# A transformer block on one core: QKV products in the score banks, paired rests, a third w1 buffer and first loads from two queues

## The chip, the cores and the metric

The kernel runs on one core of one Trainium2 chip. The metric is the device time of one execution in microseconds. Engines are called PE or TensorE (matmuls), DVE or VectorE, ACT or ScalarE, POOL or GpSimd, and SP or SyncE, which issues the transfers (DMAs).

## The reference

One block on x of shape (1, 2048, 576) in bfloat16: an attention part with 32 heads of 18 columns and a compressive memory, then a feed-forward part of 4608 columns, both on a layer norm and both added to their input.

```python
x = A_x
h = x + attention(layernorm(x), wq, wk, wv, wo, beta)
h2 = h + (gelu(layernorm(h) @ w1 + b1) @ w2 + b2)

# attention: 4 segments of 512 tokens, one after the other, per head
p = softmax(q k^T * scale + causal mask)            # inside the segment
a_dot = p @ v
a_mem = (phi(q) @ M) / (phi(q) @ z + 1e-6)          # phi(t) = t + 1 if t > 0 else exp(t)
o = sigmoid(beta) * a_mem + (1 - sigmoid(beta)) * a_dot
M += phi(k)^T @ v;  z += sum(phi(k))                # for the segments to come
return o @ wo
```

## The kernel before

The 2048 tokens are cut into 16 tiles of 128, and these into eight chunks of two tiles (`NCH`, `c`; a tile is `t = 2 * c + tl`). Two chunks are one segment. The work stands in streams, written as Python generators:

- `stream_P(tl)`: loads x, layer norm, transpose to `xT`, products with `wqkv` (576 rows, 1728 columns, resident), copies out of PSUM to `qk_pad` and `v_aug`, transposes to `QT` and `KT`. From chunk 1 on the 1728 columns are cut into four of 432 (`CH`). Each product sums over 576 rows in five matmuls, four of 128 rows (`mm5`, line 612) and a rest of 65 rows (64 and a row of zeros, line 613).
- `stream_M`: phi(k) with v into the memory (line 799).
- `stream_A`: 80 visits. A visit computes 16 score matmuls of 32 rows, four at a time in the array (line 841), into the four banks of `st4`; one exp over all 2048 columns on ScalarE (line 847); a causal mask; then attention with v into the bank `ox` (line 873, four column tiles). The memory's part is line 910.
- `stream_B(tl)`: transposes the attention's output, product with `wo_t`, adds x, layer norm, transposes to `xn2T` (four buffers of one chunk), and writes h plus b2 to DRAM.
- `stream_F1`: for each chunk nine groups of 512 columns of w1. The rest of 64 rows goes first, as tails in two row halves (line 1185), then four 128-row matmuls each (line 1198). Line 1208 on VectorE or line 1206 on ScalarE adds b1, line 1220 is GELU on ScalarE. Chunk 0's first five groups go by half chunks (lines 1158 and 1160; `xz` holds rows padded with zeros).
- `stream_F2`: 36 matmuls of 288 columns for each half tile (line 1254), then the sum with h (line 1258) and the store.

PSUM has eight banks: four for the scores (`st4`), `ox`, and three small ones (`bank_slots`) that all other products share. When the scores are done, all eight are for F1 and F2.

The weights w1 don't stay on chip. Each group (512 KB and two rests of 32 KB) is loaded anew for each chunk, into two buffers, `w1_bufs`, in turn. For chunk 0 three more lie in the second `hT` buffer, and late in the kernel three lie in `wqkv`.

```python
w1_at = {n: ("w1m", n % 5) if n < NG and n % 5 > 1 else ("w1", n % 5 if n < NG else (n - NG) % 2) for n in range(W1Q)}
```

What runs when is not left to a scheduler at run time. Each operation is recorded with `op(engine, duration, issue, reads, writes)`; `either` names two engines that could do it. The list `ORDER` (written out, from a search by a planner with costs and due times that stands in the same file) gives the order in which all operations are issued, and with a minus sign the second engine of an `either`. `PLACE` gives the small bank of each use. Each engine runs its own queue in this order and waits where data are not there, so nothing overtakes a waiting instruction on its engine. All transfers are issued by SyncE in this kernel, the first loads too (lines 531 to 535: x, then wk, beta, wq, wv).

At the start, before the first product, TensorE runs small matmuls on zeros (line 1326). The transposes of the first tiles are line 657, the product that spreads the gate beta over the partitions is line 550, and the copy of `xT` out of PSUM is line 692.

## Time and profile before

| what | value |
| --- | --- |
| time before, median of 3 runs | 460.34 us (458.75 to 461.04) |
| the profiled execution: its time, its span | 458.34 us, 456.6 us |
| TensorE busy | 448.5 us, 98% of the span |
| ScalarE, VectorE, GpSimd busy | 69%, 63%, 32% |
| mean DMA rate | 183 GB/s |
| granted TensorE clock | 1.00 |

The span runs from the first to the last instruction of one execution; all rows of the profile are from that execution. In a timeline's row the first number is the start in us, the second the length, then engine, line, operation and tiles, with a count of merged instructions; in brackets stands the idle time before it and what ended it. In a row of a group the numbers behind the bar are the busy time, the mean length of one in ns, and the idle time before.

### The profile page before, as it was taken

Reading aid. Unit: us, or ns where it says so; the run is one execution under the profiler, and the core shown is the slowest. Engines: PE = TensorE matmul, PEld = TensorE weight load, DVE = VectorE, ACT = ScalarE, POOL = GpSimd, SP = SyncE. Lnnn points to the kernel's source line nnn. Section 1 sums busy time; section 2 is a strip of 40 time slices with the busy share of each in tenths; the row PEclk is TensorE's granted clock in tenths of the full one; section 3 lists DMA queues with packets and bytes.
Section 4 is the critical chain, followed back from the end, with each engine's and each line's share of the span. In section 5 each row is a group of like instructions: output and inputs, shape, how many; then the busy total and the mean of one; then the engine's idle time right before and its main releaser. Section 6 shows DMA issues by size and latency. Waiting matters only on the chain.

```text
span 456.6 us, 14417 instructions
## 1 busy us (share of the span) xinstructions
PE 448.5 (98%) x6074; PEld 333.2 (73%) x6074; DVE 286.9 (63%) x761; ACT 315.3 (69%) x316; POOL 147.4 (32%) x202
## 2 busy tenths in 40 slices
PE   7999999999999999999999999999999999999997
PEld 5776776666777777776567777667788888888874
DVE  6998888887786767876765686678672532211101
ACT  5999889976887965797786876978932354366230
POOL 4776423564373033436512333233210020000000
PEclk9999999999999999999999999999999999999999
DMA  7989998969798987787796679987778767575001
GB/s 227 329 252 264 193 184 201 182 176 178 166 251 156 232 202 178 195 177 135 204 176 165 180 194 165 201 201 156 192 193 213 196 194 191 161 208 157 27 14 39
DMA packets 137491, 83.39 MB, mean 183 GB/s; under 512 B 72786, under 2 KB 135634, under 8 KB 137426
## 3 DMA queue, kind: packets, MB, share of 16 engines
q1 hardware_dynamic: 137426, 82.47, 76.5%
q8 instruction: 47, 0.77, 0.7%
q14 instruction: 18, 0.15, 0.1%
HBM read 59.43 MB, written 6.49 MB: 144 GB/s over the span
## 4 chain that ended last, share of the span: by engine, by line
PE 89%; DMA 5%; SPq 3%; ACT 1%; DVE 1%; issue 1%; ACTq 0%
PE bank L1254 21%; PE bank L1198 17%; PE bank L612 13%; PE late L1254 6%; PE late L1198 6%; PE st L841 5%; PE ox L873 4%; PE bank L613 3%; PE bank L1185 3%; PE bank L1158 2%; PE ox L1254 1%; PE ox L1198 1%; SPq L367 1%; DMA hT<-in_B_w_dram 1%; DMA w1g<-in_B_w_dram 1%; DMA beta_row<-in_A_beta_dram 1%
## 5 line engine op out<-in xcount | busy, mean ns | idle before, releaser
L847 ACT ACTIVATE pt<-st 128x2048 bf16<-128x2048 f32 x80 | 150.1, 1877 | 41.9 <-PE st L841 21.2
L1254 PEld LDWEIGHTS <-hT 128*128 128x128 bf16 x1152 | 109.4, 98 | 29.6 <-issue 0.8
L1254 PE MATMUL bank<-w_sb,hT 128*128 128x288 bf16 x864 | 126.3, 286 | 0.0
L1198 PE MATMUL bank<-xn2T,w1g 128*128 128x256 bf16 x656 | 85.3, 273 | 0.0
L852 POOL TENSOR_SCALAR_AFFINE_SELECT pt<-pt 128x512 bf16<-128x512 bf16 x81 | 52.4, 658 | 95.2 <-ACT pt L847 88.8
L1198 PEld LDWEIGHTS <-w1g 128*128 128x128 bf16 x768 | 71.4, 98 | 16.2 <-issue 6.1
L1208 DVE TENSOR_TENSOR hT<-bank,b1T 128x512 bf16<-128x512 f32 x70 | 47.3, 685 | 41.5 <-PE bank L1198 41.1
L1220 ACT ACTIVATE hT<-hT 128x1536 bf16<-128x1536 bf16 (+3 forms) x24 | 65.7, 2768 | 0.2
L612 PE MATMUL bank<-wqkv,xT 128*128 128x432 bf16 (+1 forms) x268 | 57.1, 336 | 0.9 <-DMA xT<-xn 0.8
L612 PEld LDWEIGHTS <-xT 128*128 128x128 bf16 x400 | 36.9, 97 | 19.8 <-DMA xT<-xn 0.9
L1206 ACT ACTIVATE hT<-late,b1T 128x256 bf16<-128x256 f32 x32 | 13.3, 477 | 38.7 <-PE late L1198 22.3
L1258 DVE TENSOR_TENSOR ot<-bank,hc 128x288 bf16<-128x288 f32 x24 | 11.0, 456 | 43.0 <-PE bank L1254 38.0
L1206 ACT ACTIVATE hT<-bank,b1T 128x256 bf16<-128x256 f32 x56 | 23.5, 473 | 20.1 <-PE bank L1198 20.1
L1254 PE MATMUL late<-w_sb,hT 128*128 128x288 bf16 (+1 forms) x216 | 33.9, 296 | 0.0
L841 PE MATMUL st<-QT,KT 32*128 32x128 bf16 x1280 | 32.4, 217 | 0.5 <-issue 0.5
L841 PEld LDWEIGHTS <-KT 32*128 32x128 bf16 x1280 | 18.7, 92 | 15.2 <-issue 11.9
L1198 PEld LDWEIGHTS <-wqkv 128*128 128x128 bf16 x272 | 26.0, 98 | 4.6 <-issue 0.8
L854 DVE TENSOR_TENSOR pt<-pt,causal 128x512 bf16<-128x512 bf16 x47 | 22.4, 479 | 8.3 <-ACT pt L847 8.1
L646 POOL TENSOR_TENSOR rstd_b<-rstd_b,mhalf 128x1 f32<-128x1 f32 x16 | 9.3, 582 | 56.2 <-DVE rstd_b L636 53.8
L873 PE MATMUL ox<-pt,v_aug 128*32 128x128 bf16 x1184 | 26.3, 221 | 0.0
L873 PEld LDWEIGHTS <-v_aug 128*32 128x32 bf16 x1184 | 17.2, 96 | 10.6 <-issue 8.2
L613 PE MATMUL bank<-wqkv,xT 65*128 65x432 bf16 (+1 forms) x67 | 22.6, 338 | 0.0
(156 smaller groups left out, 642.0 us busy)
## 6 DMA issues: line engine op xcount, KB each, us to landing
w1g<-in_B_w_dram SPq DMA_DIRECT2D x50, 512.0 KB, 4.1
wqkv<-in_B_w_dram SPq DMA_DIRECT2D x17, 512.0 KB, 3.9
w_sb<-in_B_w_dram SPq DMA_DIRECT2D x6, 864.0 KB, 7.7
hd<-h_t SPq DMA_DIRECT2D x14, 288.0 KB, 4.2
hc<-hd SPq DMA_DIRECT2D x28, 144.0 KB, 2.9
w1g<-in_B_w_dram SPq DMA_DIRECT2D x100, 32.0 KB, 3.2
x_b<-in_A_x_dram SPq DMA_DIRECT2D x18, 144.0 KB, 3.0
hT<-in_B_w_dram SPq DMA_DIRECT2D x5, 512.0 KB, 6.0
```

Of the source, the lines that this page charges most:

```text
L612: nc.tensor.matmul(out=out_ap, lhsT=lhsT_of(slice(0, P), k), rhs=rhs_of(slice(0, P), k), start=(k == 0), stop=False)
L613: nc.tensor.matmul(out=out_ap, lhsT=lhsT_of(slice(0, KTAIL), 4), rhs=rhs_of(slice(0, KTAIL), 4), start=False, stop=True)
L841: nc.tensor.matmul(out=st4[:, i, n * P:(n + 1) * P], lhsT=KTs[(c - c % 2 + kt // 2) % 3][rows, g, (kt % 2) * P:(kt % 2 + 1) * P], rhs=QTs[ ...
L847: op("ACT", 1.88, lambda: nc.scalar.activation(out=pt[:], in_=st4[:], func=ACT.Exp, scale=scale), sk, [("pt", slot, n) for n in range(4)], ...
L852: either(("POOL", 0.64, lambda part=part: nc.gpsimd.affine_select(out=part, in_=part, pattern=[[0, 4], [1, P]], compare_op=ALU.is_ge, fill ...
L854: ("DVE", 0.42, lambda part=part: nc.vector.tensor_tensor(out=part, in0=part, in1=causal[:].unsqueeze(1).to_broadcast([P, 4, P]), op=ALU.m ...
L873: nc.tensor.matmul(out=ox[32 * i:32 * i + 32, g % 4 * P:(g % 4 + 1) * P], lhsT=v_flat[(2 * s0 + kt) % 6][:, h * E:h * E + 32], rhs=pts[slo ...
L1198: nc.tensor.matmul(out=bank(b)[:, a * Q:(a + 1) * Q], lhsT=w1_main(wt)[:, k, (2 * (h % 2) + a) * P:(2 * (h % 2) + a + 1) * P], rhs=xn2T[c ...
L1206: nc.scalar.activation(out=hT[:, f + a, :], in_=bank(b)[:, a * Q:(a + 1) * Q], func=ACT.Identity, bias=b1T[:, f + a:f + a + 1])
L1208: either(("DVE", 0.69, lambda hT=hT, f=f, b=b: nc.vector.tensor_tensor(out=hT[:, f:f + 2, :], in0=bank(b)[:].rearrange("p (a w) -> p a w", ...
L1220: op("ACT", (f1 - f0) * Q * 0.00083 + 0.18, lambda hT=hT, f0=f0, f1=f1: nc.scalar.activation(out=hT[:, f0:f1, :], in_=hT[:, f0:f1, :], fun ...
L1254: nc.tensor.matmul(out=acc, lhsT=hT[:, q, tl * P:(tl + 1) * P], rhs=w2_sb[:, q, hs], start=(q == 0), stop=(q == NF - 1))
```

## The change

1. From chunk 3 on (`PAIRED`), the QKV product of a tile takes the four score banks instead of four uses of small banks. The rests come first: four matmuls of 64 rows, on the lower and the upper partitions in turn, so that two use different halves of the array. For this, two DMAs copy 64 rows of `wqkv` to the upper partitions for two of the four cuts, and the layer norm writes the last 64 columns twice. `BEFORE` names the visit ahead of which each tile's product stands.
2. A third buffer for w1 (`w1_bufs`). To make room, `xn2T` goes from four buffers to three, and `beta_row`, `ones`, `b1_rows` and `xz` lie in `t1` and `t2`, which are used later.
3. The first loads may be issued by SyncE or ScalarE (`dma_two`); wq, wk and wv come in halves of 288 columns.
4. A new `ORDER` and `PLACE`. In it ScalarE issues five loads: the first x, the last rows of wq, beta, one half of wq and one of wk.

When the scores are done, the score banks and `ox` now join the small banks at places that `PLACE` gives.

The diff, without `ORDER`, `PLACE` and renamed keys:

```diff
+    def dma_two(kb, issue, rd=(), wr=(), slack=0.0):
+        o = either(("SP", 0.5, lambda: issue(nc.sync)), ("ACT", 0.55, lambda: issue(nc.scalar)), rd, wr, slack)
...
-    w1_bufs = [sbuf(f"w1g{j}", [W1]) for j in range(2)]
+    w1_bufs = [sbuf(f"w1g{j}", [W1]) for j in range(3)]
-    xn2T = [sbuf(f"xn2T{j}", [KT, Q]) for j in range(4)]
+    NX = 3
+    xn2T = [sbuf(f"xn2T{j}", [KT, Q]) for j in range(NX)]
+    early = t1[:].rearrange("p h e -> p (h e)").bitcast(BF16)
+    ones, beta_row, b1_rows = early[:, 0:P], early[:, P:P + H], early[:, 2 * P:3 * P]
+    xz = t2[:].rearrange("p h e -> p (h e)").bitcast(BF16)[:, 0:2 * Q].rearrange("p (h q) -> p h q", h=2)
...
-        weights(wqkv, slice(j * D, (j + 1) * D), W, f"wqkv{j}")
+        for h in range(2):
+            to = slice(j * D + h * HALF, j * D + (h + 1) * HALF)
+            dma_two(290, lambda e, to=to, h=h, W=W: e.dma_start(
+                out=wqkv[:, 0:4, to], in_=W[0:512, h * HALF:(h + 1) * HALF].rearrange("(k p) n -> p k n", p=P)), (), [f"wqkv{j}{h}"])
...
+    PAIRED = 3
+    BEFORE = {6: 22, 7: 23, 8: 27, 9: 38, 10: 45, 11: 47, 12: 52, 13: 55, 14: 62, 15: 64}
...
+            if (c, tl) == (PAIRED, 0):
+                yield need(lambda: (PAIRED - 1, 0) in half_V and (PAIRED - 1, 1) in half_V, idle=False)
+                for lo, hi in ((CH, 2 * CH), (3 * CH, 4 * CH)):
+                    dma(55, lambda lo=lo, hi=hi: nc.sync.dma_start(out=wqkv[64:P, 4, lo:hi], in_=wqkv[0:64, 4, lo:hi]),
+                        [f"wqkv{j}t" for j in range(3)], ["wqkv_pad"])
...
+            paired = c >= PAIRED
+            if paired:
+                yield need(lambda: visited[0] >= BEFORE[t] and all(u in projected for u in BEFORE if u < t), st_slots, [kx] + every, mode=64)
+                st = st_slots.take()
+                def rests(xTt=xTt, cuts=cuts):
+                    for i, (lo, hi) in enumerate(cuts):
+                        rows = slice(64 * (i % 2), 64 * (i % 2) + 64)
+                        nc.tensor.matmul(out=st4[:, i, 0:hi - lo], lhsT=xTt[rows, 4, :], rhs=wqkv[rows, 4, lo:hi], start=True, stop=False,
+                                         skip_group_check=True)
+                op("PE", 2 * mm(CH), rests, [kx] + every, [st], n=8, mode=64)
...
+                    for k in range(4):
+                        nc.tensor.matmul(out=area()[:, 0:hi - lo], lhsT=xTt[:, k, :], rhs=wqkv[:, k, lo:hi], start=False, stop=(k == 3),
+                                         skip_group_check=True)
...
-    w1_at = {n: ("w1m", n % 5) if n < NG and n % 5 > 1 else ("w1", n % 5 if n < NG else (n - NG) % 2) for n in range(W1Q)}
+    w1_at = {n: ("w1m", n % 6) if n < NG and n % 6 > 2 else ("w1", n % 6 if n < NG else n % 3) for n in range(W1Q)}
```

More of the change, by code (lines that the diff above doesn't have):

```diff
@@ L517, in swap @@
         for i in range(4):
-            banks["st", i] = pool.tile([P, 512], F32, name=f"late{i}")
+            banks["bank", 3 + i] = pool.tile([P, 512], F32, name=f"late{i}")
+        banks["bank", 7] = ox
     bank_slots.free.append("ox")
@@ L834, in scores @@
         own = 2 * (c % 2) + qt
-        sk = [("st", i) for i in range(4)]
+        st = st_slots.take()
+        sk = [st]
         def go():
@@ L1002, in stream_A @@
                             done_A.add(c)
-        bank_slots.free.append("ox")
-        st = [("st", i) for i in range(4)]
-        op("POOL", 0.0, swap, (), st, slack=-1000, port=False)
-        bank_slots.free += st
+        more = [("bank", 3 + i) for i in range(5)]
+        used = [("pt", slot, n) for slot in range(2) for n in range(4)] + [("v", t, j) for t in (2, 3) for j in range(2)]
+        op("POOL", 0.0, dynamic_swap, used, ["ox"] + more, slack=-1000, port=False)
+        bank_slots.free += more
         late.append(True)
```

125 lines of the change are left out of this document (74 added, 51 removed), and 230 rows, old and new, of the table ORDER.

## The prediction

> **What bounds the kernel now.** I read the page's engine table and chain first, then busy time by stretches, then TensorE's timeline around the places that the change touches, then single groups of instructions.
>
> ```profile
> span 456.6 us, 14417 instructions
> PE 448.5 (98%) x6074; PEld 333.2 (73%) x6074; DVE 286.9 (63%) x761; ACT 315.3 (69%) x316; POOL 147.4 (32%) x202
> PE 89%; DMA 5%; SPq 3%; ACT 1%; DVE 1%; issue 1%; ACTq 0%
> ...
> core 0: us, PE busy (x) PEld busy (x) DVE busy (x) ACT busy (x) POOL busy (x), PEclk, DMA share, GB/s
> 0.00:20.00 20.00, 17.68 (x186) 13.12 (x187) 15.45 (x52) 14.46 (x26) 11.52 (x24) 1.00 0.89 271
> ...
> 200.00:240.00 40.00, 38.36 (x619) 26.09 (x617) 27.70 (x76) 33.20 (x33) 17.28 (x22) 1.00 0.83 179
> 240.00:280.00 40.00, 40.00 (x547) 30.08 (x545) 27.55 (x70) 30.14 (x26) 13.21 (x20) 1.00 0.67 174
> ```
>
> TensorE is busy 448.5 of 456.6 us, carries 89% of the chain, and has stretches with no gap at all (240 to 280). No other engine passes 69%. So the time is TensorE's own work plus the few places where it waits. An edit is worth what it takes from one of these two; a faster copy or transfer elsewhere is worth nothing by itself. Busy time hides what a matmul really occupies, because matmuls overlap; I take the distance from one start to the next:
>
> ```profile
> 117.23 0.40 PE L841 MATMUL st<-QT,KT 32*128 32x128 bf16 x16
> 117.56 0.41 PE L873 MATMUL ox<-pt,v_aug 128*32 128x128 bf16 x16
> 117.91 0.39 PE L1185 MATMUL bank<-xn2T,w1g 64*128 64x256 bf16 x4
> 118.23 1.92 PE L1198 MATMUL bank<-xn2T,w1g 128*128 128x256 bf16 x16
> 119.99 0.89 PE L612 MATMUL bank<-wqkv,xT 128*128 128x432 bf16 x4
> 120.72 0.35 PE L613 MATMUL bank<-wqkv,xT 65*128 65x432 bf16 x1
> 120.90 0.89 PE L612 MATMUL bank<-wqkv,xT 128*128 128x432 bf16 x4
> 121.63 0.35 PE L613 MATMUL bank<-wqkv,xT 65*128 65x432 bf16 x1
> 121.91 0.63 PE L873 MATMUL ox<-pt,v_aug 128*32 128x128 bf16 x32
> ```
>
> A full 432-column matmul occupies 0.73/4 = 0.18 us (119.99 to 120.72), and the rest of the contraction, with 65 rows, just as much: 0.18 us (120.72 to 120.90). A 256-column one takes 1.76/16 = 0.11 us (118.23 to 119.99). The four tails of 64 rows, in two row halves, take 0.32 us (117.91 to 118.23): two times 0.11 and 0.10 over, so the halves do run together and the change of tile shape costs 0.10. The other way it costs the same: 121.63 + 0.18 = 121.81, and the next shape starts at 121.91.
>
> **Rests as row pairs.** Of 16 token tiles, the ten of chunks 3 to 7 change. Each had four rests of 0.18 us; now two pairs: 10 x 2 x 0.18 = 3.6 us less. But the pairs stand in a shape of their own. In the order of instructions of the two built programs I count 278 changes of shape before and 296 after, everything counted: 18 more, at 0.10 to 0.12 us each (the upper end from the 16 scores, 0.33 us, of which four times half of 0.11 are streaming) 1.8 to 2.2, taken 2.0. Net 1.6 us less. All of this is on the path, since TensorE has no idle time to hide it in.
> The Trainium skill, "TensorEngine Tiling (Array Packing)", section "Tiling Modes", says that changing the tiling mode drains TensorE; this speaks against pairs in small groups, and the trace agrees, with 0.10 us. Its page "TensorE: Matmul & The Clock Gate", section "Single matmul latency", puts a drain at about 175 ns; an estimate from that page would charge 18 x 0.175 = 3.2 us and leave 0.4 us of the gain. The measured row decides.
>
> **Products in the score banks.** Each paired tile takes all four score banks: 2 x 0.18 + 4 x 0.73 = 3.3 us of products, then five copies out. Until the last copy no scores may be issued, and TensorE takes its queue in order.
>
> ```profile
> L847 ACT ACTIVATE pt<-st 128x2048 bf16<-128x2048 f32 x80 | 150.1, 1877 | 41.9 <-PE st L841 21.2 <-PE ox L873 13.1 <-issue 1.8
> L1220 ACT ACTIVATE hT<-hT 128x4608 bf16<-128x4608 bf16 x10 | 40.1, 4039 | 0.1
> L711 DVE CAST qk_pad<-bank 128x432 bf16<-128x432 f32 x16 | 9.7, 604 | 4.4 <-PE bank L613 4.2
> L710 ACT CAST v_aug<-bank 128x432 bf16<-128x432 f32 x7 | 3.7, 525 | 0.5 <-PE bank L613 0.5
> L1208 DVE TENSOR_TENSOR hT<-bank,b1T 128x512 bf16<-128x512 f32 x70 | 47.3, 685 | 41.5 <-PE bank L1198 41.1 <-ACT pt L847 0.2
> ```
>
> The products finish 0.73 us apart and a copy takes 0.52 (ScalarE) or 0.60 (VectorE), so after the last product one copy, about 0.7 us with its hand-over, is left when its engine is free. In the new order the shortest work between the last product and the next scores is 1.7 us (tile 7: eight matmuls of F2, four tails, 16 of attention; tile 12 much the same), elsewhere 2.1 to 6. I cost it at nothing; the cover is that work, 1.0 us more than needed. If it is gone (a 4.04 us GELU or one 0.69 us eviction ahead of the copy), each tile loses up to 4.04 + 0.52 - 1.7 = 2.9 us: a rival below. On the gain side three small banks, freed of 40 projections, wait less; TensorE's waits on banks are too small now to price, so that stays at nothing.
>
> **Third buffer.** TensorE's waits on transfers after the start are these:
>
> ```profile
> 76.62 0.39 PE L1185 MATMUL bank<-xn2T,hT 64*128 64x256 bf16 x4
> 77.42 1.92 PE L1198 MATMUL bank<-xn2T,hT 128*128 128x256 bf16 x16 [0.40 <-DMA hT<-in_B_w_dram]
> ...
> 148.19 0.66 PE L612 MATMUL bank<-wo_t,xT 128*128 128x288 bf16 x4 [0.30 <-DMA xT<-o_nat]
> ...
> 216.09 0.90 PE L612 MATMUL bank<-wqkv,xT 128*128 128x432 bf16 x4 [0.77 <-DMA xT<-xn]
> ...
> 239.43 0.39 PE L1185 MATMUL bank<-xn2T,w1g 64*128 64x256 bf16 x4 [0.88 <-DMA w1g<-in_B_w_dram]
> ...
> w1g<-in_B_w_dram SPq DMA_DIRECT2D x50, 512.0 KB, 4.1
> ```
>
> The first and last are w1: 0.40 + 0.88 = 1.3 us. With two buffers a load starts when the group two back is done; with three it has a whole group more, against 4.1 us to landing. I take both as gone. Bounds: 0 (the load is late because SyncE issues it late, behind others in its queue, which no buffer cures) to 2.4 us (the two xT waits, 1.07, go too). What is late next is an xT transpose on the same queue. The price of the buffer, one xn2T fewer, is nothing: by the new order the chunk whose buffer is reused has ended its F1 at least 60 us of TensorE work earlier. The same for xz, ones, beta and b1 rows that now lie in t1 and t2: the last read of xz stands 12 us of TensorE work ahead of chunk 2's first memory product, whose result overwrites it. A second small VectorE operation for each of ten layer norms is off the path (63% busy).
> Two added copies on chip put the weights of every second rest on the upper partitions. The second is the 67th transfer of SyncE's new queue; in the old one, issues 67 to 71 run as follows:
>
> ```profile
> 68.51 0.59 SPq L1105 DMA_DIRECT2D hT<-in_B_w_dram  x1
> ...
> 71.72 0.43 SPq L1105 DMA_DIRECT2D hT<-in_B_w_dram  x1
> ...
> 71.72 5.66 DMA hT<-in_B_w_dram
> ```
>
> The first rests come about 75 us in, by the new order's TensorE work ahead of them and the 8 us that the old trace had lost by then. Issued at 68.5 to 71.7, the copy lands with the last row's 5.66 us at 77.4 at the latest: a single wait of 0 to 2.4 us, and I take 0.4, since it is a tenth of that row's 512 KB.
>
> **First loads from two queues.**
>
> ```profile
> 0.79 1.28 ACT L593 ACT_TABLE_LOAD   x1 [0.79 <-PEq L1370]
> 0.80 0.87 SPq L531 DMA_DIRECT2D x_p<-in_A_x_dram  x2
> 1.71 0.43 SPq L534 DMA_DIRECT2D wqkv<-in_A_wk_dram  x1
> 3.09 0.82 DVE L622 BATCH_NORM_STATS2 stats_p<-x_p 128x6 f32<-128x288 bf16 x2 [0.38 <-DMA x_p<-in_A_x_dram]
> 5.53 0.69 ACT L692 COPY xT<-ox 128x640 bf16<-128x640 bf16 x1 [1.01 <-PE ox L657]
> 7.00 0.17 PE L550 MATMUL bank<-beta_row,ones 1*128 1x32 bf16 x1 [0.21 <-DMA beta_row<-in_A_beta_dram]
> 7.50 0.65 PE L612 MATMUL bank<-wqkv,xT 128*128 128x288 bf16 x4
> 10.22 0.36 PEld L612 LDWEIGHTS <-xT 128*128 128x128 bf16 x4 [0.41 <-DMA wqkv<-in_A_wq_dram]
> ```
>
> xT is ready at 6.2 us (5.53 + 0.69), but the first product starts at 7.50: the gate's small product waits ahead of it for beta, whose load stands behind 576 KB of wk. In the new order beta is ScalarE's third issue, and wq comes in halves on both queues. New limit: ScalarE issues five loads (0.43 each, like SyncE's), the fifth once the first x has landed (3.1), to 3.5; then the 1.28 table load, a 0.3 copy, and xT at 5.5 to 6.2 as before. The transposes may be some 0.4 later, as two x loads now share the engines from the start. First product at about 6.7: 0.8 us less. Bounds: a loss of 0.5, if wq's first half lands late, to a gain of 1.3.
> The Trainium skill, "DMA: Bandwidth & Descriptors", section "Issuing engines are not separate DMA queues", says that issuing from several engines saves issue time only. The first 20 us here are busy by 0.89 on the transfer engines at 271 GB/s, which leaves little beyond issue and order; by that rule alone the head would give nothing.
>
> **The sum.** 456.6 - 3.6 + 2.0 - 1.3 + 0.4 - 0.8 = 453.3 us of span. The profiled execution took 458.34 us, 1.74 more than its span, so 455.0; it ran 2.0 under the median of 460.34, so on the median's scale **457.0 us**, 0.7% less. About 0.5%, 2.3 us, is what can be told from no change: 458.0 and 462.6 are the bounds.
>
> **Rivals.** *Gains eaten by the feeds.* The w1 waits turn into others of the same size on SyncE's one queue, and the head stays bound by bytes: 456.6 - 1.6 + 0.4 = 455.4, on the median's scale 459.1, no change. For it: SyncE's queue is in order, and the head's transfers are at 0.89. Against it: the 1.3 us at the head were order (beta), not bytes. 0.20.
> *Late copies hold the score banks: slower.* Place: the scores after each of the ten projections. It decides from 0.6 us a tile on: the forecast is 3.3 under before, 2.3 over is slower, 5.6/10. With 0.9 lost a tile, 453.3 + 9 = 462.3, on the median's scale 466.0. For it: one late copy stops all of TensorE, and the new ScalarE order puts GELUs of 4 us ahead of copies of several tiles. Against it: most tiles have 2 to 6 us of cover, and now TensorE waits little for 80 exps of 1.88 us in the same banks. 0.15.
> *The pairs don't overlap*, both halves reading one at a time: 3.6 back, 460.2, no change. The tails' 0.32 us speaks against it. 0.02.
>
> **How the numbers follow.** Forecast 0.63, of which 0.58 lies under 458.0 and the rest just above, where the head's loss or the full wait for the copy would put it; the first rival, 1.1 above the bound, adds 0.04 to faster. Faster 0.62, same 0.23, slower 0.15. Downward the head can give 0.5 more, the waits 1.1, the shapes 0.2 and the copy 0.4, 2.2 in all, and the lowest of the runs shown (458.75) lies 1.6 under the median: 457.0 - 3.8 = 453.2. Upward I reach past the first rival to the second with 0.5 lost a tile: 457.0 + 5 = 462.0. Range 453.2 to 462.0.
>
> **What would show it.** Right: rests in groups of four with 0.36 us and a change of about 0.10 on each side; 80 scores that start without idle time behind the projections; no TensorE wait on w1 over 0.3 us; the first product before 7 us. Wrong: TensorE idle ahead of scores, put down to a copy from the score banks; idle time of over 1.5 us in any stretch that is full now; a first product after 7.5.

## The result, and the profile after: slower by 0.9%

| | before | after |
| --- | --- | --- |
| median of 13 runs each, same chip | 459.94 us (458.47 to 463.53) | 464.69 us (462.21 to 466.5) |
| ratio after to before, 95% interval | | 1.0092 (1.0065 to 1.0119) |
| span of the profiled execution | 456.6 us | 463.4 us |
| idle gaps of TensorE over 0.02 us, with 1.9 to 2.0 at the start, summed from the trace | 5.4 us | 11.3 us |

457.0 was forecast, with a range of 453.2 to 462.0: the time lies above the range, on the other side of no change. Ratios and their intervals are of the fast runs alone: of the twelve runs each of item 13, its sibling and item 15 below, three, one and two lie over 1.5% above the fastest and are left out there, but not of the medians. In the page of the changed kernel (engines' busy time, then the shares of the chain that ended last) TensorE is as busy as before, in a span 6.8 us longer (4.75 us by the medians: the execution profiled before ran 1.6 us under its median, the one after 0.4 over), and the chain runs through ScalarE and VectorE for 3% each instead of 1%:

```profile
span 463.4 us, 14374 instructions
PE 448.6 (97%) x6067; PEld 331.1 (71%) x6067; DVE 287.8 (62%) x772; ACT 313.8 (68%) x305; POOL 154.3 (33%) x209
PE 85%; DMA 6%; ACT 3%; DVE 3%; SPq 2%; issue 1%; POOL 0%; ACTq 0%; DVEq 0%
```

What TensorE waited for in the changed kernel (sum in us, times, longest):

```profile
PE bank L1245 <- DMA w1g<-in_B_w_dram: 2.1, 2, 1.1
PE bank L1386 <- DVE pq L581: 1.9, 1, 1.9
PE st L895 <- ACT qk_pad L731: 1.6, 2, 1.0
PE bank L1258 <- DMA w1g<-in_B_w_dram: 1.2, 1, 1.2
PE st L895 <- ACT v_aug L731: 1.2, 2, 1.0
PE st L743 <- ACT pt L901: 0.9, 1, 0.9
PE st L743 <- DMA wqkv<-wqkv: 0.7, 1, 0.7
```

L895 is the scores, L743 the paired rests, L1245 and L1258 the first layer's tails and main matmuls, L731 the copies out of the score banks; L1386 is the wait at the very start, 2.0 before. So 2.8 us are scores that stand behind copies, 3.3 us are waits for first-layer weights (1.3 before), 0.7 is the on-chip copy of `wqkv`, and 0.9 is tile 9's rests, which need the score banks that an exponential is still reading.

One more cost stands in no wait of TensorE. The last sum of the feed-forward part, before and after:

```profile
453.93 0.31 DVE L1258 TENSOR_TENSOR ot<-ox,h_t 128x144 bf16<-128x144 f32 x1 [0.49 <-PE ox L1254]
```

```profile
460.03 0.61 DVE L1318 TENSOR_TENSOR ot<-late,h_t 128x432 bf16<-128x432 f32 x1 [1.79 <-PE late L1314]
```

The new order ends with the wider of two pieces, 432 columns and not 144. From the start of this sum to the end of the span it is 3.4 us, before 2.7. These 0.7 us are in the profile of every version with the new order (3.3 to 3.4 us).

The copies, at tile 12, first on TensorE:

```profile
222.19 0.54 PE L743 MATMUL st<-wqkv,xT 64*128 64x432 bf16 x4
222.66 3.09 PE L763 MATMUL st<-wqkv,xT 128*128 128x432 bf16 x16
225.59 0.44 PE L852 MATMUL bank<-v_aug,phik_pad 128*128 128x76 bf16 x8
...
226.71 0.63 PE L928 MATMUL ox<-pt,v_aug 128*32 128x128 bf16 x32
228.36 0.40 PE L895 MATMUL st<-QT,KT 32*128 32x128 bf16 x16 [1.02 <-ACT qk_pad L731]
```

The four rests take 0.47 us with their change of shape (222.19 to 222.66), as forecast. The products end at 225.6. The copies of ScalarE and of VectorE in the same stretch:

```profile
225.79 0.52 ACT L731 CAST qk_pad<-st 128x432 bf16<-128x432 f32 x1 [3.15 <-PE st L763]
226.98 0.28 ACT L731 CAST v_aug<-st 128x144 bf16<-128x144 f32 x1 [0.68 <-DVE v_aug L732]
227.79 0.52 ACT L731 CAST qk_pad<-st 128x432 bf16<-128x432 f32 x1 [0.52 <-DVE qk_pad L732]
```

```profile
226.34 0.61 DVE L732 CAST v_aug<-st 128x432 bf16<-128x432 f32 x1 [2.07 <-ACT qk_pad L731]
227.30 0.46 DVE L732 CAST qk_pad<-st 128x288 bf16<-128x288 f32 x1 [0.35 <-ACT v_aug L731]
```

Two things are to be seen. The first copy starts 0.2 us after the last product, although the first product was done 2.2 us earlier. And each copy begins 0.03 us after the other engine's copy has ended, and names it as its releaser: five copies on two engines run as one chain of 2.5 us. In the ten tiles the copies end 2.4 to 4.1 us after the last product; the scores stand idle at four of them (0.97 us at tile 7, 0.21 at 8, 1.02 at 12, 0.62 at 13).

The first products:

```profile
5.40 0.71 PE L670 MATMUL ox<-ident,xn 128*128 128x128 bf16 x5 [0.52 <-DVE xn L641]
...
7.01 1.16 PE L625 MATMUL bank<-wqkv,xT 128*128 128x288 bf16 x4
...
8.74 1.16 PE L625 MATMUL bank<-wqkv,xT 128*128 128x288 bf16 x4
...
9.94 0.72 PE L625 MATMUL ox<-wqkv,xT 128*128 128x288 bf16 x4
```

The first starts at 7.01, 0.49 sooner than before. But four matmuls take 1.16 us where they took 0.65, half the rate, so the third product starts at 9.94, against 8.73 before.

### The profile page after: what moved, and what is told of

Read it like the earlier page. It is cut to its first block, busy times and chain, and to the rows that moved or that the text cites. A ratio compares the mean times of both kernels' runs of the same rounds, so it can differ in the third digit from the quotient of the medians.

```text
span 463.4 us, 14374 instructions
## 1 busy us (share of the span) xinstructions
PE 448.6 (97%) x6067; PEld 331.1 (71%) x6067; DVE 287.8 (62%) x772; ACT 313.8 (68%) x305; POOL 154.3 (33%) x209
## 4 chain that ended last, share of the span: by engine, by line
PE 85%; DMA 6%; ACT 3%; DVE 3%; SPq 2%; issue 1%; POOL 0%; ACTq 0%; DVEq 0%
PE bank L1314 20%; PE bank L1258 16%; PE bank L625 6%; PE late L1258 6%; PE st L895 5%; PE st L763 5%; PE ox L1314 5%; PE ox L928 4%; PE late L1314 4%; PE bank L1245 3%; DMA w1g<-in_B_w_dram 2%; PE bank L1217 2%; DMA o_col<-oT 2%; ACT pt L901 2%; PE bank L626 2%; DMA wqkv<-wqkv 1%
## 5 line engine op out<-in xcount | busy, mean ns | idle before, releaser
L1314 PE MATMUL bank<-w_sb,hT 128*128 128x288 bf16 x792 | 115.7, 286 | 0.5 <-DVE hT L1268 0.5
L1258 PE MATMUL bank<-xn2T,w1g 128*128 128x256 bf16 x680 | 88.2, 273 | 1.2 <-DMA w1g<-in_B_w_dram 1.2
L1258 PEld LDWEIGHTS <-w1g 128*128 128x128 bf16 x816 | 75.8, 98 | 17.7 <-issue 4.8
L907 POOL TENSOR_SCALAR_AFFINE_SELECT pt<-pt 128x512 bf16<-128x512 bf16 x75 | 48.7, 663 | 74.9 <-ACT pt L901 72.3
L1266 ACT ACTIVATE hT<-bank,b1T 128x256 bf16<-128x256 f32 x48 | 20.2, 475 | 24.7 <-PE bank L1258 24.6
L895 PE MATMUL st<-QT,KT 32*128 32x128 bf16 x1280 | 32.2, 216 | 3.0 <-ACT qk_pad L731 1.6
L763 PE MATMUL st<-wqkv,xT 128*128 128x432 bf16 x160 | 32.5, 346 | 0.0
L895 PEld LDWEIGHTS <-KT 32*128 32x128 bf16 x1280 | 19.2, 92 | 16.8 <-issue 13.3
L625 PEld LDWEIGHTS <-xT 128*128 128x128 bf16 x240 | 22.9, 99 | 8.6 <-ACT xT L713 0.2
L1268 DVE TENSOR_TENSOR hT<-late,b1T 128x512 bf16<-128x512 f32 x16 | 10.9, 686 | 28.7 <-PE late L1258 28.7
L1314 PE MATMUL ox<-w_sb,hT 128*128 128x288 bf16 x180 | 27.9, 286 | 0.0
L1314 PE MATMUL late<-w_sb,hT 128*128 128x288 bf16 (+2 forms) x180 | 27.1, 286 | 0.0
L1258 PEld LDWEIGHTS <-wqkv 128*128 128x128 bf16 x240 | 23.0, 98 | 4.1 <-issue 0.6
L1115 POOL TENSOR_TENSOR h_t<-h_t,b_bc 128x576 f32<-128x576 f32 x16 | 20.6, 1290 | 12.3 <-DVE r L989 8.9
```

The source lines that it names most:

```text
L625: nc.tensor.matmul(out=out_ap, lhsT=lhsT_of(slice(0, P), k), rhs=rhs_of(slice(0, P), k), start=(k == 0), stop=False)
L763: nc.tensor.matmul(out=area()[:, 0:hi - lo], lhsT=xTt[:, k, :], rhs=wqkv[:, k, lo:hi], start=False, stop=(k == 3), skip_group_check=True)
L895: nc.tensor.matmul(out=st4[:, i, n * P:(n + 1) * P], lhsT=KTs[(c - c % 2 + kt // 2) % 3][rows, g, (kt % 2) * P:(kt % 2 + 1) * P], rhs=QTs[ ...
L907: either(("POOL", 0.64, lambda part=part: nc.gpsimd.affine_select(out=part, in_=part, pattern=[[0, 4], [1, P]], compare_op=ALU.is_ge, fill ...
L1258: nc.tensor.matmul(out=bank(b)[:, a * Q:(a + 1) * Q], lhsT=w1_main(wt)[:, k, (2 * (h % 2) + a) * P:(2 * (h % 2) + a + 1) * P], rhs=xn2T[c ...
L1266: nc.scalar.activation(out=hT[:, f + a, :], in_=bank(b)[:, a * Q:(a + 1) * Q], func=ACT.Identity, bias=b1T[:, f + a:f + a + 1])
```

## The experiments

Ratios are to the kernel before, run on the same chip beside each, with 95% intervals; a point is 0.01 of the ratio, 4.6 us. Two kernels' ratios differ reliably only by 0.4 points or so. Line numbers in edited kernels are 16 or 17 higher, since the list `ORDER` takes more lines. The letters of theories are explained in each expectation; from item 9 on E stands for the one queue that weights and transposes share.

**1 and 2. Five copies from one tile or from four.** A small kernel: 24 rounds of four products and of the changed kernel's copies, alternating engines. They differ in this:

```diff
-    one = ps.tile([P, 4, 512], F32, name="one")
-    area = lambda i: one[:, i, 0:432]
+    tiles = [ps.tile([P, 512], F32, name=f"t{i}") for i in range(4)]
+    area = lambda i: tiles[i][:, 0:432]
```

> A small kernel of its own: 24 rounds of four products of 4x432 columns into four banks that are declared as one tile, and the same five copies as the changed kernel's, handed in turn to ScalarE and VectorE. It leaves out everything else of the computation. Theory 'in series' (two reads of one declared tile wait for each other although they are in different banks): a VectorE copy begins only after the ScalarE copy before it has ended, by 0.03 us as in the changed kernel's trace, so a round's five copies take the sum of their times, 0.52 + 0.61 + 0.28 + 0.46 + 0.52 = 2.4 us. Rival 'side by side' (the waits in the changed kernel come from what else the two engines do): the copies of ScalarE and VectorE overlap and a round's copies are over in 1.2 to 1.4 us.

> The same small kernel, with the four banks declared as four tiles of one bank each; nothing else differs. Theory 'in series': now the copies of the two engines overlap, a round's five copies are over in 1.2 to 1.4 us after its last product, and the first of them begin while products still run. Rival 'side by side': no difference between this kernel and the one with one tile.

With one tile, ScalarE, VectorE and TensorE:

```profile
49.49 0.52 ACT L46 CAST qk<-one 128x432 bf16<-128x432 f32 x1 [4.91 <-PE one L43]
50.69 0.40 ACT L48 CAST qk<-one 128x288 bf16<-128x288 f32 x1 [0.68 <-DVE va L47]
51.76 0.28 ACT L50 CAST va<-one 128x144 bf16<-128x144 f32 x1 [0.68 <-DVE qk L49]
```

```profile
50.04 0.61 DVE L47 CAST va<-one 128x432 bf16<-128x432 f32 x1 [5.77 <-ACT qk L46]
51.12 0.61 DVE L49 CAST qk<-one 128x432 bf16<-128x432 f32 x1 [0.47 <-ACT qk L48]
```

```profile
44.63 4.76 PE L43 MATMUL one<-w,xa 128*128 128x432 bf16 x16 [2.70 <-ACT va L50]
52.09 4.54 PE L43 MATMUL one<-w,xa 128*128 128x432 bf16 x16 [2.70 <-ACT va L50]
59.33 3.08 PE L43 MATMUL one<-w,xa 128*128 128x432 bf16 x16 [2.69 <-ACT va L50]
```

With four tiles, ScalarE, then VectorE:

```profile
43.67 0.40 ACT L48 CAST qk<-t 128x288 bf16<-128x288 f32 x1 [1.58 <-PE t L43]
43.97 0.29 ACT L50 CAST va<-t 128x144 bf16<-128x144 f32 x1
45.13 0.52 ACT L46 CAST qk<-t 128x432 bf16<-128x432 f32 x1 [0.88 <-PE t L43]
```

```profile
44.35 0.61 DVE L47 CAST va<-t 128x432 bf16<-128x432 f32 x1 [2.44 <-PE t L43]
44.87 0.60 DVE L49 CAST qk<-t 128x432 bf16<-128x432 f32 x1
```

"In series" holds. From one tile, five copies take 2.55 us end to end (49.49 to 52.04), and TensorE stands idle for 2.70 us in each round. From four tiles the two engines overlap, each copy waits only for its product, some run while TensorE's products do (41.96 to 45.04), and its idle time is 0.48 us a round. The rounds differ by more than that, 7.46, 7.24 and 5.77 us in turn against 3.56, since two of three rounds of the first kernel also run in part at half rate (4.76 and 4.54 us of products, against 3.08). The TensorE rows show why the copies cannot come earlier either: the next round's first product, into a bank that was the first to be read out, waits 2.70 us for the last copy of another bank. Here what is declared as one tile is one resource. I didn't declare the score banks as four tiles in the changed kernel itself: that its copies are a chain for this reason is read from the same hand-overs of 0.03 us. The Trainium skill, "PSUM — Partial Sum Buffer", section "PSUM bank collisions raise a hardware error", asks for a guard by bank and quadrant only; with four tiles the waits agree with that, with one tile they go further.

**3. One copy instead of five** (the rest of q, k and v from chunk 3 on is not brought out).

```diff
+                skip = c >= PAIRED and ch > 0
-                either(("ACT", ..., lambda: nc.scalar.copy(out=dst, in_=src())),
+                either(("ACT", ..., lambda: None if skip else nc.scalar.copy(out=dst, in_=src())),
```

> The changed kernel with four of the five copies out of the score banks left out in each of its ten paired tiles (only the first 432 columns are copied; the rest of q, k and v from chunk 3 on is not brought out). Theory A (the scores wait for the five copies, 2.82 us of idle TensorE before four tiles' scores, each gap costing some 0.25 us more than the record shows): those four gaps go, and the span falls by 2.8 to 4 us, to 459.4 to 460.6. Rival B (the late first-layer weights set the time, and the score gaps only take up slack that would show elsewhere): the gaps go but the next wait for weights grows by as much, and the span stays above 462.4.

Span 459.5, median 461.22, ratio 1.0038 (1.0012 to 1.0064): 0.54 points less, 2.5 us. The four score gaps are gone. Not all of the span's 3.9 us is theirs: the third product started at 8.70 here (1.2), and one wait for weights grew from 0.99 to 1.92, after which the clock stood at 0.50 from 140.4 to 143.8. So theory A holds, with some of it given back to the weights. The edit also takes 40 copies of 0.3 to 0.6 us off ScalarE and VectorE, so the 2.5 us need not all be the scores'; item 5 keeps the copies.

**4. TensorE busy until the first transposes.**

```diff
         for o in arranged():
-            o.issue()
+            for again in range(5 if o.made == 89 else 1):
+                o.issue()
```

> The changed kernel with one of its warm-up matmuls issued five times instead of once, so that TensorE is busy from 4.5 to 5.4 us where it now stands idle between its 13th warm-up and the first transposes (4.68 to 5.40). Theory C (the idle stretch is why the first products run at 240 ns a matmul until 9.9 us, where the kernel before has 120 ns from 5.9 us on): the 120 ns spacing begins by about 6 us, the first product takes 0.6 instead of 1.2 us, the third product starts at 8.3 to 8.6 instead of 9.94, and the span falls by 1.3 to 1.6 us. Rival D (the slow spacing comes from the weights still landing, or from loads issued by ScalarE): the spacing stays 240 ns until 9.9 us and the span does not move.

```profile
5.53 0.48 PE L686 MATMUL ox<-ident,xn 128*128 128x128 bf16 x5
...
6.80 0.66 PE L641 MATMUL bank<-wqkv,xT 128*128 128x288 bf16 x4
...
7.70 0.65 PE L641 MATMUL bank<-wqkv,xT 128*128 128x288 bf16 x4
...
8.45 0.66 PE L641 MATMUL ox<-wqkv,xT 128*128 128x288 bf16 x4
```

In this execution the full rate is there from the transposes on, as theory C has it. Its size was wrong: ratio 1.0085 (1.0060 to 1.0110), median 462.84, only 0.07 points. The profiles of the other runs tell why. With the idle stretch the third product starts at 9.94, 8.70, 8.94, 8.41, 8.42, 8.42 and 8.48 (the changed kernel and the runs of items 3, 5, 6, 8, 9 and 14), mean 8.76; with it filled, at 8.41 to 8.97, mean 8.62 in eight runs; and in the kernel before at 8.73, and at 8.41 in item 10. The profiled execution of the changed kernel was the worst draw. Nor is the idle stretch shown to be the cause: of the seven executions with it four run the first product at the full rate (0.66 us, items 6, 8, 9 and 14), and of the eight without it one doesn't (0.81 us, item 15). The Trainium skill, "TensorE: Matmul & The Clock Gate", section "What's actually happening", says that the rate doubles after a busy window of about 3.4 us that runs freely, so that the onset varies by some 0.5 us. The trace agrees that it varies, but by more: here the full rate comes between 6.75 (or sooner) and 10 us.

**5. Copies on one engine, with cover.**

```diff
-  ORDER: copies of tiles 7, 8, 12, 13 in turn on ScalarE and VectorE;  774 (scores) ... 728 ... 731;  1699 (scores), 1315
+  ORDER: all of them on ScalarE;                                       728, 731, 774;               1315, 1699
```

> The changed kernel with the copies of tiles 7, 8, 12 and 13 all handed to ScalarE and three pieces of feed-forward work put ahead of the scores that stood idle (two of 0.43 us at tile 7, one of 0.47 us at tile 12); all of the computation stays. Theory A (the scores wait for copies that end 2.4 us and more after the last product): a chain on one engine goes every 0.41 us instead of 0.55 to 0.64, so the copies end 0.4 us sooner, and with the cover the idle time before these scores falls from 2.82 to about 1 us; the span falls by 1.5 to 2.2 us from 463.4. Rival B (that idle time is slack against the weights): it falls as much, but the span by under 0.5 us.

Ratio 1.0064 (1.0039 to 1.0088), median 462.70, span 459.9. No score gap is left. 0.28 points, 1.3 us, lie just under A's 1.5 to 2.2 and within what two ratios can differ by chance; 1.0 of the span's 3.5 us is the start (third product at 8.94). The waits for weights stayed (1.21, 1.61, 0.70).

**6 and 7. Five transfers earlier, alone and with 4 and 5.**

```diff
-  ORDER: 500 ... 520 ... 598 ... 519 ... 597 (on-chip copy) ... 531;      967 ... 968;    983 ... 981 ... 982
+  ORDER: 500, 597 ... 520, 519 ... 598, 531;                              967, 968;       983, 982 ... 981
```

> The changed kernel with five transfers put earlier in SyncE's queue: the second on-chip copy of the projection weights right behind the first's neighbours (60.9 instead of 72.9 us), two main loads of first-layer weights at 65 and 67 instead of 70.4 and 73.5, a tail load at 124.9 instead of 138.2, and one at 137 instead of 147.5, each behind the last reader of what it overwrites. Theory B (these loads were given late places in the queue, long after their buffer was free): the idle times of TensorE for weights at 74.94, 142.18 and 153.00 (3.29 us) and for the on-chip copy at 77.99 (0.66) go, and the span falls by 3 to 4 us. Rival E (the transfers are slow because the DMA engines are shared, so that earlier places only push others back): the sum of waits for weights stays above 2 us, and the span falls by under 1.5 us.

> The changed kernel with the three edits together: TensorE kept busy from 4.5 to 5.4 us, copies of tiles 7, 8, 12 and 13 on ScalarE with three pieces of feed-forward work ahead of the scores, and five transfers earlier in SyncE's queue; all of the computation stays. If the three causes are separate, their gains add: 1.5 to 2.5 for the first products, 1.5 to 2.2 for the copies, 3 to 4 for the loads, so the span is 455 to 457.5, below the 456.6 of the kernel before or level with it, and the median 456.5 to 459. If they hide behind one another, it stays above 460.

The first gave 1.0165 (1.0135 to 1.0195), 467.19; the three edits together 1.0114 (1.0084 to 1.0145), 465.14. The second stayed above 460 us, which its expectation gave as the sign of causes that hide behind one another. Theory B's remedy made it worse: in the first no wait for weights is left, and others have come. VectorE around 71 us in the changed kernel, and the same instruction with the early loads:

```profile
70.84 0.25 DVE L988 RECIPROCAL r<-o_col 128x16 f32<-128x16 bf16 x1 [0.18 <-DMA o_col<-oT]
```

```profile
73.57 0.25 DVE L1004 RECIPROCAL r<-o_col 128x16 f32<-128x16 bf16 x1 [4.50 <-DMA o_col<-oT]
73.74 0.36 DVE L925 TENSOR_TENSOR pt<-pt,causal 128x512 bf16<-128x512 bf16 x1
```

TensorE, in the changed kernel and with the early loads:

```profile
74.94 1.92 PE L1258 MATMUL bank<-xn2T,w1g 128*128 128x256 bf16 x16 [1.22 <-DMA w1g<-in_B_w_dram]
```

```profile
74.16 0.24 PE L944 MATMUL ox<-pt,v_aug 128*32 128x128 bf16 x4 [2.74 <-DVE pt L925]
...
75.98 3.60 PE L1274 MATMUL bank<-xn2T,w1g 128*128 128x256 bf16 x16
```

The engines' busy time with the early loads from 74.4 to 81.0 us (the third number from the right is the granted clock):

```profile
74.40:81.00 6.60, 6.39 (x42) 3.16 (x43) 6.00 (x18) 5.97 (x3) 2.06 (x3) 0.50 0.18 32
```

Two 512 KB loads now stand ahead of the attention's transpose, which lands 2.7 us later; VectorE waits 4.50 us for it in order, the causal mask stands behind that, and TensorE behind the mask: 2.74 us. Then 16 matmuls that take 1.92 us run in 3.60, under a granted clock of 0.50. Here an idle stretch of 2.7 us is paid a second time, in half-rate work after it.

**8. Rests unpaired, in the score banks** (the on-chip copies left out).

```diff
-                op("PE", 2 * mm(CH), rests, [kx] + every, [st], n=8, mode=64)
+                op("PE", 2 * mm(CH), lambda: None, [kx] + every, [st], n=8, mode=64)
...
-                    if not paired:
+                    if True:
                         mm5(area()[:, 0:hi - lo], lambda r, k: xTt[r, k, :], lambda r, k: wqkv[r, k, lo:hi])
```

> The changed kernel with the rests of the ten paired tiles computed as the kernel before does, each as a fifth matmul of its product, but still in the score banks; the two on-chip copies of the projection weights are left out, since nothing reads them. Theory A with the prediction's price of pairs (40 rests at 0.18 us against 10 groups of four at 0.36 us plus 18 more changes of tile shape at 0.11 us): TensorE's own work grows by 1.6 us, the wait for the on-chip copy (0.66 and 0.25 us) goes, and the span rises by 0.5 to 1 us with the score gaps as they are. Rival F (the change of tile shape at the pairs is what costs the time): the span falls by 1 us or more.

Ratio 1.0120 (1.0097 to 1.0144), median 465.49: 0.28 points more than the changed kernel, 1.3 us. It points the way that the prediction had it, but lies within the intervals; rival F, a gain of 1 us or more, has nothing for it. TensorE was busy for 449.6 us in its profile, 1.0 more where 1.6 was expected, and the span, which was expected to rise, was 462.9.

**9 and 10. No main loads of first-layer weights from the tenth group on**, in the changed kernel and, as control, in the kernel before.

```diff
-        dm(512, lambda e: e.dma_start(out=w1_main(wt), ...), (), [k], SLACK["w1"])
+        dm(512, lambda e: e.dma_start(out=w1_main(wt), ...) if n < 9 else None, (), [k], SLACK["w1"])
```

> The changed kernel with the main loads of the first-layer weights left out from the tenth group on (63 of 72; the products run on what lies in the buffers), so that nothing waits for them and the other transfers have the queue to themselves. It bounds what all feeding of weights costs. Theory E (the late places of these loads and the transposes' places behind them in one queue are two sides of one cost, as the run with five early transfers showed): the waits for weights (3.29 us and 0.66) go and the transposes land sooner, so that the stall behind the exponential (0.91) goes too; the scores' stalls behind the copies (2.82) stay; the span falls by 4 to 6 us, to 457.5 to 459.5. Rival B2 (the weights' waits only fill time that another chain sets): it falls by under 2 us.

> The kernel before with the same main loads of first-layer weights left out as in the run of the changed kernel without them (63 of 72; its products run on what lies in the buffers). The changed kernel fell by 1.15 points of the ratio without them (1.0092 to 0.9977). If feeding costs the changed kernel more than it cost the kernel before (the prediction's term for the third buffer has the wrong sign), this one falls by no more than its own waits for weights and the transposes behind them, 1.3 to 2.5 us, to a ratio of 0.995 to 0.997. If feeding costs both the same, it falls by 5 us, to 0.989, and the loss of the changed kernel lies with the copies and the first products alone.

Changed: 0.9977 (0.9952 to 1.0003), median 459.10, 1.15 points less. Before: 0.9926 (0.9899 to 0.9954), median 456.49, 0.74 points less. The control fell between the two expectations. Feeding costs both kernels, by these ratios 5.3 and 3.4 us; the difference of 0.41 points (1.9 us) is what the change may have added, with an uncertainty as large as itself. The fall of the changed kernel is the one that theory E had, but its rows explain less of it: 2.0 of the 3.3 us of waits for weights and the 0.9 behind the exponential are gone in the profile, while 1.3 for one of the nine groups that are still loaded, and the on-chip copy's 0.7, stayed.

**11, 12 and 13. Orders mended by hand.** Item 4 and 5's edits with one exponential ahead of another wait (11, transfers as in the changed kernel), the same with four early transfers (12); then VectorE's reciprocals behind what does not need them at two places, with a main load early (13).

```diff
-  ORDER: 1119, 1144 (exp);                                          510 (reciprocal) ... 563 (mask) ... 612;   1033, 1034 ... 1264
+  ORDER: 1144, 1119 in 11 and 12; 563 ... 612, 510 in 13;           1264, 1033, 1034 in 13
```

> The changed kernel with TensorE kept busy from 4.5 to 5.4 us, with the copies of tiles 7, 8, 12 and 13 on ScalarE and three pieces of feed-forward work ahead of the scores, and with one change of ScalarE's order: the exponential that holds the score banks before tile 9's rests goes ahead of the elu exponential that waits for VectorE. All transfers stay where the changed kernel has them. Theory A+C: of the idle time, the four score stalls (2.82) and the wait of tile 9's rests (0.91) are gone, the waits for weights stay at 3 to 4; the span is 458 to 460.5 and the ratio to the kernel before 1.002 to 1.006. If waits for weights take up what is freed: above 462.

> The kernel of the run above with four transfers placed by hand, none of them a main load that comes ahead of an attention transpose by less than 4 us: the second on-chip copy at 60.9, one main load at 65, a tail load at 124.9, and two tail loads ahead of a key transpose that waits for the scores. Theory E: the waits at 74.94, 77.99, 142.18 and 153.00 shrink from 3.95 to under 1.5 us and no transpose lands later than in the changed kernel, so the span is 2 to 3 us below the run above, 455.5 to 458, and the ratio to the kernel before under 1.000. Rival (any early load pushes a transpose back): VectorE or ScalarE again waits over 2 us for a transpose, and the span is that of the run above or longer.

> The changed kernel with TensorE kept busy from 4.5 to 5.4 us, the copies of tiles 7, 8, 12 and 13 on ScalarE with three pieces of feed-forward work ahead of the scores, and with VectorE's order mended at two places where a reciprocal that waits for a transpose of the attention's output stood ahead of a causal mask, evictions and the elu sum (it goes behind them); of the transfers, the second on-chip copy at 60.9, one main load at 65, three tail loads earlier, and a main load behind the transpose of the normalized tile. Theory E (early loads only push transposes back, and TensorE pays where VectorE stands behind a late transpose in its order): with that order mended the loads can go early without a price; no idle time above 1.3 us is left between 60 and 160 us, no stretch of half-rate matmuls follows, the span is 455.5 to 458 and the ratio 0.995 to 1.001. If it stays above 1.004, the transfers' queue itself is the bound there.

Ratios: 11 1.0048 (1.0018 to 1.0078), 12 1.0059 (1.0032 to 1.0086), 13 0.9985 (0.9955 to 1.0015). In 11 the score stalls and the rests' stall are gone, and one wait for weights grew to 2.07 us with half-rate matmuls behind it; its ratio is in the expected range, the profiled span (463.6) is not. In 12 no wait for weights is left, but one of 1.59 us for a transpose and one of 0.98 for a mask, with half-rate matmuls behind the mask (74.3 to 77.6 us, clock 0.50): 12's expectation of 2 to 3 us below 11 fell. In 13, median 460.21, the changed kernel is level with the kernel before, as expected, though idle times of 1.09 and 1.45 us are left. A sibling of 13 with the main load at 69.8 us gave 1.0005 (0.9978 to 1.0032), median 459.91:

> The kernel of the run above, with its early main load at 69.8 instead of 65 (in front of one tail load only, behind the transpose of the attention's output). Theory E: TensorE waits 0.4 to 0.9 us for that load at 73 to 75 us and the transpose lands at 70.8 as in the changed kernel; the span is within 1 us of the run above.

TensorE waited 3.12 us for that load, more than expected, and the median was level all the same.

**14 and 15. Reciprocals late everywhere**, alone in the changed kernel (26 places), and with the edits of 13.

```diff
-  ORDER: reciprocal (988), product (989), masks, evictions, sums ..., product that needs them (994)
+  ORDER: masks, evictions, sums ..., reciprocal (988), product (989), product that needs them (994)
```

> The changed kernel with one edit: on VectorE, the reciprocal that waits for the transpose of the attention's output, and the small product behind it, stand right ahead of the one instruction that needs them (26 places) and no longer ahead of masks, evictions, statistics and elu sums. VectorE waited 9.7 us in all at that reciprocal in the changed kernel, and under 1 us in the kernel before. Theory E (late transposes cost TensorE through VectorE's order): TensorE's wait for the exponential at 147.73 (0.91) goes, and the waits behind evictions that runs with other DMA timing show (0.5 to 1.5 us at 72 to 92) become rare; the median falls by 1 to 2 us and the ratio to 1.005 to 1.007. Rival G (VectorE's waits there are off the path): the ratio stays at 1.009.

> All edits of order together: TensorE busy from 4.5 to 5.4 us, the copies of four tiles on ScalarE with three pieces of work ahead of the scores, the reciprocals late on VectorE at all places, and the transfers of the run that put a main load at 65 us, with two more tail loads of 45 KB earlier. The run without the last two edits of this list had the ratio 0.9985. Theory E: the stalls left in its profile (1.09 us for a tail load at 78.35 and 1.45 us behind VectorE at 91.71) go; the span is 455 to 457 and the ratio 0.993 to 0.997, faster than both kernels. Rival: new stalls of the same size, ratio 0.998 or more.

Alone: 1.0118 (1.0096 to 1.0140), median 464.29, so theory E's gain did not come; rival G. VectorE's wait for these transposes fell from 9.7 to 3.0 us (it is 1.0 in the kernel before), TensorE's stall behind the exponential went, and its waits for weights grew by as much:

```profile
PE bank L1261 <- DMA w1g<-in_B_w_dram: 3.1, 2, 1.8
...
PE bank L1274 <- DMA w1g<-in_B_w_dram: 1.0, 1, 1.0
```

All together: 0.9998 (0.9971 to 1.0026), so its expectation fell as well. I found no version that beats the kernel before.

**16. Three suspects away at once**: items 3, 4 and 9 in one kernel.

> The changed kernel with three suspects taken away at once: four of the five copies of each paired tile are left out, the main loads of first-layer weights are left out from the tenth group on, and TensorE is kept busy from 4.5 to 5.4 us. Alone these gave 0.54, 1.15 and 0.07 points of the ratio. If they are separate causes, the sum holds: 1.0092 - 0.0176 = 0.9916, somewhat below the 0.9926 of the kernel before without those loads, since the paired rests still save their 1.3 to 1.6 us. If they hide behind one another, the ratio stays at 0.995 or more, and something else in the changed kernel costs 1 us or more against the kernel before.

Ratio 0.9911 (0.9884 to 0.9937), median 456.22: the sum of the single effects, 0.9916, holds, and it is level with the kernel before without the same loads (0.9926). What TensorE still waits for:

```profile
PE bank L1403 <- DVE pq L597: 1.9, 1, 1.9
PE bank L1275 <- DMA w1g<-in_B_w_dram: 1.3, 1, 1.3
```

So beside these three the change hides no cost of much more than 2 us; the later end, 0.7 us, is one that this run kept.

## Why the prediction was wrong

**Products in the score banks: the step that failed.** It costed the move at nothing, since "after the last product one copy, about 0.7 us with its hand-over, is left", under 1.7 us of cover. That took copies to follow their products one by one and two engines to work side by side. Neither is so: five copies begin after the last product and run in one chain, 2.4 to 4.1 us against 0.7. Tile 7 and tile 12, named there as the thinnest cover, are the ones that lost most (0.97 and 1.02). Measured by leaving copies out: 0.54 points, 2.5 us, part of which the weights took back; with all copies kept but ended sooner and covered (item 5), 0.28 points, 1.3 us. The small kernels show why; the trace of before could not, since there each product had a bank that was a tile of its own.

**Third buffer: wrong sign in the profile.** -1.3 with bounds of 0 to 2.4 was forecast; the waits for weights rose from 1.3 to 3.3 us. The reason given for the bound at nothing ("the load is late because SyncE issues it late, behind others in its queue, which no buffer cures") was the right one: the tail load of a group was issued at 138.2, its sibling at 124.4.

```profile
124.40 0.48 SPq L1167 DMA_DIRECT2D w1g<-in_B_w_dram  x1
...
138.20 1.11 SPq L1167 DMA_DIRECT2D w1g<-in_B_w_dram  x2
```

But putting loads forward by hand only moved the wait onto transposes in the same queue (items 6, 7 and 12). Nor are the transfer engines busier there than before, on the mean. The stretch from 140 to 160 us, changed kernel, then before (busy us of five engines, clock, DMA share, GB/s):

```profile
140.00:160.00 20.00, 17.03 (x233) 11.79 (x232) 13.01 (x38) 16.54 (x9) 5.66 (x8) 1.00 0.82 171
```

```profile
140.00:160.00 20.00, 19.70 (x250) 15.29 (x248) 14.57 (x40) 17.94 (x11) 1.46 (x2) 1.00 1.10 210
```

The bound, as I read it, is the one order of transfers with waits in it; no run isolates that. Whether the change itself made feeding dearer stays open: 1.9 us by the controls, with an uncertainty as large. The on-chip copy cost 0.7 where 0.4 was taken, within 0 to 2.4.

**First loads: half right.** The first product came at 7.01, "before 7" was named as the sign; six other runs with this head had 6.75 to 6.91. But the gain ended at the third product: in the profiled execution the products ran at half rate until 9.9, and over all runs the third product starts where it did (mean 8.76, before 8.73 and 8.41). So -0.8 became about 0. The prediction priced when the work starts, not how fast it then runs, nor that transposes now stand ahead of the second product (8.21 us). Fewer warm-up matmuls and the idle 0.7 us ahead of the transposes may be why the rate came late; item 4 gained 0.3 us, within chance.

**Rests as row pairs: right.** The four rests take 0.36 us and a change of shape 0.11 (0.47 in all); unpaired, the kernel is 1.3 us slower, against 1.6 forecast, though the intervals don't prove it.

**The end: put at nothing.** The sum has no term for the new order's last piece, which ends the span 0.7 us later.

**The rivals and the sum.** The step of weighing failed too: "late copies hold the score banks" and "gains eaten by the feeds" were set as alternatives, with 0.15 and 0.20. Both came, and together: -1.3 for the pairs, 1.3 to 2.5 for the copies, 1.9 for the feeds, 0.3 for the idle start and 0.7 for the end make 2.9 to 4.1 us of the 4.2 measured, each but the last with 1 to 2 us of uncertainty. That the first rival's 466.0 us came near the 464.69 measured was luck: it had 9 us from 0.9 at each of ten tiles by GELUs ahead of copies, where the copies cost up to 1.0 at four tiles by their own chain. A slip that decides nothing: the pairs that don't overlap would give 457.0 + 3.6 = 460.6, not 460.2. "80 scores that start without idle time" and "no TensorE wait on w1 over 0.3 us" were the signs named, and both are broken in the profile.

## What to carry to other kernels

Before two engines are counted as working side by side on PSUM, look at what is declared as one tile: here copies from four banks of one tile ran in one chain, and even a product into a bank already read waited for the last of them. A move that keeps TensorE's work but makes it wait for a buffer in common is priced by the whole chain that frees it, against the thinnest cover, and several small costs are added up, not set against each other. A transfer put forward in a queue in order is paid by what stands behind it, so a wait that goes in one row must be looked for in the next.

## What the runs showed that I had not expected

Idle time of TensorE can be paid twice. After 2.74 us of idle the next 16 matmuls of 256 columns took 3.60 instead of 1.92 us (item 6), and the granted clock stood at 0.50 for 6.8 us. In items 3, 11, 12 and 16 there are stretches of 3.4 us at 0.50. In the small kernel with 2.70 us of idle in every round 16 matmuls of 432 columns took 4.76, 4.54 and 3.08 us in turn, against 3.08 in every round with 0.48 us of idle. The Trainium skill, "TensorE: Matmul & The Clock Gate", section "What's actually happening", names an idle window of about 3.4 us for this; here less was enough.

The length of one idle stretch doesn't decide it. In item 12 two gaps of 0.98 and 0.53 us within 2.3 us were enough (the next 16 took 3.56 us); after one gap of 1.22 us in the changed kernel the rate was full (1.92 us), and so it was after the longest in the sibling of item 13:

```profile
75.25 1.92 PE L1274 MATMUL bank<-xn2T,w1g 128*128 128x256 bf16 x16 [3.12 <-DMA w1g<-in_B_w_dram]
```

What decides stays open. Nor is this all of the spread between runs: item 13's version ran between 456.43 and 465.43 us (the kernel before beside it between 457.62 and 462.2), and of its three slowest runs two had a mean clock of 0.996 over the run and one 1.00.
